# Second mlp: row transposes by VectorE blocks and a DMA through DRAM, in place of TensorE

## The chip, the cores and the metric

The kernel runs on one core of a Trainium2 chip. The metric is the device time of one launch, in microseconds (us). TensorE (PE) does matrix products into PSUM, VectorE (DVE), ScalarE (ACT) and GpSimd (POOL) do elementwise work, and SyncE (SP) issues all DMAs, in the order of its own instruction list. Every engine takes its instructions in order and waits on semaphores for the others.

## The reference

An attention between 512 sequence rows and 32 state rows of each of 8 batch entries makes 8 x (512 + 32) = 4352 token rows of 512 numbers. They pass through two mlps:

```python
def _moe_ref(x, w_gate, w_val, w_out):
    gate = 1.0 / (1.0 + np.exp(-(x @ w_gate)))
    return (gate * (x @ w_val) @ w_out).astype(np.float32)      # 512 -> 1536 -> 512

def _moe2_ref(x, w_in, w_out, g_ln):
    h = x @ w_in                                                # 512 -> 1024
    h_max = np.max(h, axis=-1, keepdims=True)
    e = np.exp(h - h_max)
    sm = e / (np.sum(e, axis=-1, keepdims=True) + 1e-09)
    solu = h * sm
    mu = np.mean(solu, axis=-1, keepdims=True)
    var = np.mean((solu - mu) ** 2, axis=-1, keepdims=True)
    ln = (solu - mu) / np.sqrt(var + 1e-06) * g_ln
    return (ln @ w_out).astype(np.float32)                      # 1024 -> 512
```

Weights and g_ln arrive as float64, and the kernel converts them on the chip.

## The kernel before

Float32 products run as three passes: each operand is split into a high half (a rounded copy) and a low half (the operand less the high half), and `mm3` (L131) sums high x high, low x high and high x low in PSUM. So every matrix product costs three matmuls, and every operand costs one copy for the high half (`hi_of`, ACT, L123) and one subtraction for the low half (`lo_of`, DVE, L129).

Up to about 750 us the kernel does attention, the first mlp (batch row by batch row, in 12 chunks of 128 hidden columns) and the conversion of all weights. Its results, transposed (features on the partitions), go to DRAM (`ysp`). In the last batch row the weights `w_out2` are converted and multiplied by g_ln (`Conv`, L894 and L895).

The second mlp runs over 34 tiles of 128 token rows (`tiles`, L580: eight batch entries of 4 tiles and 2 tiles of state rows). For each tile i:

- `h2` (L610): 24 matmuls of 512 columns for h = x @ w_in, into two of four PSUM banks `acc`, and a DVE maximum of each half.
- `chain` (L616): ACT takes exp of both halves (L621), DVE multiplies by h (L624), makes the statistics (L625, L626) and subtracts the mean (L627) in the tile `eb[i % 3]`. The tile has tokens on the partitions.
- `trans` (L644): the product with `w_out2` needs features on the partitions. Eight TensorE transposes of 128 x 128 (L648) go to the PSUM banks `gps` and `vps`; ACT and DVE split each into high and low halves (`uhl`: the tiles woh9 to woh11, wol9 to wol11, xe2 and xo2).
- `row_scale` (L629): some small DVE operations and two small POOL operations make one factor for each row.
- `out2` (L653): 24 matmuls of 512 columns into `att[i % 2]`; `store` (L661) scales and writes the result.

The loop at L952 issues h2 of tile i, then trans of tile i - 1, chain of tile i, and out2 and store of tile i - 2. Beside it the inputs of the next batch entry are loaded from `ysp` (`y_load`, L590) and split (`y_split`, L595), four pieces for each group of four tiles. In this last loop a scheduler sets the order of each engine's instructions from its own estimate of times; the order is fixed when the kernel is built.

Of the kernel before, what the change touches and what calls it, by code (L numbers as in the profile page):

```python
# [8 lines left out]
F32 = mybir.dt.float32  # L9
# [6 lines left out]
P = 128  # L16
STAGES = 10
WARM = 11
EXPS = 7
# As float32 patterns: float64 high words of 2**-127 and of 2**128.  # L20
EXP_LO = 2.0 ** -15
# [4 lines left out]
def attn_moe_moe2_kernel(ctx: ExitStack, tc: tile.TileContext, x, state, w_gate, w_val, w_out, w_in2, w_out2, g_ln, out):  # L26
    """Float32 products run as float32r passes: each operand is split exactly into hi + lo
    (12 significant bits each) and hi*hi + hi*lo + lo*hi is accumulated in PSUM.

    The weights are float64: their words are taken apart on chip, rounded to float32 and split."""  # L30
    nc = tc.nc
# [24 lines left out]

    # matmul operands
    woh = [f32rt(f"woh{c}", C) for c in range(NF1)]
# [6 lines left out]
    gl = [f32rt(f"gl{i}", S) for i in range(2)]  # L65
    # float32 work tiles
    xn = [f32t(f"xn{g}", 1024) for g in range(2)]
# [18 lines left out]

    # gate's and val's weights of two chunks side by side: first in float32, later split
    wf, wf_pool, xe, xo = {}, {}, {}, {}
    for p in range(NF1 // 2)[::-1]:
        wf_pool[p] = ctx.enter_context(ExitStack())  # L90
        wf[p] = wf_pool[p].enter_context(tc.tile_pool(name=f"sbw{p}", bufs=1)).tile([P, KC, 2, 2, P], F32, name=f"wf{p}")

    def x_pool(p):
        sbx = ctx.enter_context(tc.tile_pool(name=f"sbx{p}", bufs=1, side="right"))
        xe[p], xo[p] = [sbx.tile([P, KC, 2, 2, P], F32R, name=f"{x}{p}") for x in ("xe", "xo")]

    # what only the first row needs
    early = ExitStack()
# [36 lines left out]

# [1 line left out]
    def win(k, f):  # L137
# [9 lines left out]
    class Conv:  # L147
        """Jobs of 512 weights a partition each: load, join the words and, for a pair of
        destination tiles, split.

        `rings` gives the staging and scratch tiles of a job."""

# [6 lines left out]
        def load(self):  # L159
            if not self.jobs:  # L160
                return
            n, src, dst, scale = self.jobs[0]
            i, s = self.rings(n)[0]
            if i in self.held:
                return
            self.jobs.pop(0)
            self.held.add(i)
            v = s.bitcast(U32)
            nc.sync.dma_start(out=v.rearrange("p (k f) -> p k f", k=KC) if len(src.shape) == 3 else v, in_=src)
            self.loaded.append((n, dst, scale))  # L170

        def take(self):
            """Of each word pair: the high word's magnitude, the low word rounded to float32's last place."""
            n, dst, scale = self.loaded.pop(0)
# [14 lines left out]
        def bits(self, n=1):  # L189
            """The high word as float32's bits, kept within float32's range of exponents."""  # L190
            jobs = self.taken[:n]
            for _, _, _, _, t, _, _ in jobs:
                vec.tensor_scalar(out=t, in0=t, scalar1=EXP_LO, scalar2=EXP_HI, op0=ALU.max, op1=ALU.min)  # L193
            for _, _, _, _, t, _, _ in jobs:
                tu = t.bitcast(U32)
                vec.tensor_scalar(out=tu, in0=tu, scalar1=3, scalar2=0x3FFFFFFF, op0=ALU.logical_shift_left, op1=ALU.bitwise_and)  # L196

        def sign(self, n=1):
            """The high word's sign and upper exponent bit."""
            jobs, self.taken = self.taken[:n], self.taken[n:]  # L200
# [37 lines left out]

# [1 line left out]
    def stf(a):  # L240
# [21 lines left out]
    def load_xq(a, g):  # L262
        """x in 32 x 32 blocks, for the transposes of the Vector engine."""
        for q in range(2):
# [8 lines left out]
    def a_state_mm(a, o):  # L273
        """The states transposed, head pairs block diagonal."""
        for j in range(4):
            nc.tensor.transpose(o[:, 64 * j:64 * j + 64], stf(a)[:, j, :], ident[0:64, 0:64])
# [12 lines left out]
    def a_state_pair_split(a, o):  # L289
        if paired(a) and a % 2 == 0:  # L290
            # side by side, in turn the one row's and the other's first
            v = o.rearrange("p (r k e n) -> p r k e n", r=2, k=2, e=2)
# [23 lines left out]
    def a_scores_t(a, g, o, xt):  # L316
        """With the sequence on the partitions."""
        for q in range(2):
# [6 lines left out]

    # softmax over the states, of 16 rows a partition
    def rows_t(g):
# [25 lines left out]
    def a_cols(g):  # L353
        # softmax over the sequence
        m = st2[g]
# [12 lines left out]
    def exps():  # L368
        for g in range(2):
            rows_exp(g)  # L370
        for g in range(2):
            a_cols_exp(g)
        # brings the sigmoid's table back before it is waited for
        act(stat[0][:, 0:1], half, AF.Sigmoid)
# [27 lines left out]
    def a_sread_scale(o):  # L402
        """For probabilities not divided by their sums yet."""
        for g in range(2):
# [27 lines left out]
    def attention(a):  # L432
        """Attention of batch row a by chunks: what the Tensor engine does, and what the others do after it."""
        o = att[1 - a % 2]
# [36 lines left out]

# [1 line left out]
    def ps_acc(m, n):  # L473
        return acc[m][:, 0:n]

    # Of a batch row, xread @ w is taken as attention @ (state @ w), with state @ w = [head and state, ff].
    def put(src, h, l, hi=hi_of):
# [19 lines left out]
    def state_w(b, p, g, i, o, hi, o2=vps):  # L497
        """Of two chunks, half of the heads."""
        n = 2 * p + g
# [6 lines left out]
        elif b % 2 == 0:  # L506
            # the next row's go to DRAM until it is their turn
            for q, o in enumerate((gps, o2)):
# [15 lines left out]
    def state_w1(c, o=gps, t=slice(0, 2), hi=hi_of):  # L524
        """Of one chunk for the first row, all heads, to the ring's first two."""
        p, e = divmod(c, 2)
# [10 lines left out]
    def first_mm(b, c, t, i, parts=range(2)):  # L537
        """From the operands i and i + 1 of the ring for a batch row, from the weights for the state's part."""
        o = (gps, vps)[t]
# [37 lines left out]

# [1 line left out]
    order = [B - 1, 0, SREAD] + list(range(1, B - 1))  # L579
# [15 lines left out]
    def y_split(q, k):  # L595
        n = S if order[q] < B else SR
        h, l = yhl(q, k)
        put(yf[q % 2][k][:, 0:n], h[:, 0:n], l[:, 0:n])

# [16 lines left out]
    def chain(i):  # L616
# [9 lines left out]
        vec.bn_aggr(out=s[:, 4:6], in_=s[:, 8:20])  # L626
        vec.tensor_scalar(out=u, in0=u, scalar1=s[:, 4:5], scalar2=None, op0=ALU.subtract)  # L627

    def row_scale(i):  # L629
        # r / sqrt(r^2 var + 1e-6) with r = 1 / (sum + 1e-9)  # L630
        s = stat[i % 4]
# [8 lines left out]
    def uhl(i, q):  # L640
        n = 2 * (i % 2) + q
        return (woh[9 + n], wol[9 + n]) if n < 3 else (wpart(xe, 2, 0), wpart(xo, 2, 0))

    def trans(i):  # L644
        u = eb[i % 3]
        for q, o in ((0, gps), (1, vps)):
            for j in range(4):
                nc.tensor.transpose(o[:, j * P:(j + 1) * P], u[:, (4 * q + j) * P:(4 * q + j + 1) * P], ident)  # L648
            h, l = uhl(i, q)
            hi_of(h, o)  # L650
            lo_of(l, o, h)

# [19 lines left out]

# [1 line left out]
    def job(c, t):  # L674
# [15 lines left out]

    # the operands of a batch row's gate and val, made ahead: state @ w by halves of pairs of chunks
    ring = [(b, p, g) for b in blocks[1:] if b < B for p in range(NF1 // 2) for g in range(2)]
# [10 lines left out]
    def loads(n):  # L703
        """What the next ones to be made need from DRAM."""
        nonlocal loaded
# [8 lines left out]
    def a_next(b):  # L714
        """The operand of the next block's first products."""
        if b < B:
# [8 lines left out]

    # the first row, with the weights converted just ahead of their use
    with tc.manual_schedule():
# [73 lines left out]

        # by chunk: what the Tensor engine does, and what the others do after it
        parts = [
# [25 lines left out]

        # The chunk with the exponentials keeps the Activation engine busy: its weights are taken  # L830
        # before, some of its other work is left to the next one.
        ahead = {4: 3, 5: 3, EXPS: 0}
# [53 lines left out]
    with tc.manual_schedule():  # L886
        for n_b, b in enumerate(blocks[1:], 1):
# [5 lines left out]
            if last:  # L893
                nc.sync.dma_start(out=glnt, in_=g_ln.rearrange("(j p) -> p j", p=P))  # L894
                conv = Conv([(rows(w_out2, j), (woh[j], wol[j]), glnt[:, j:j + 1]) for j in range(NF2)], rings)  # L895
                conv.load()
# [52 lines left out]
    assert not conv.jobs and not conv.loaded and not conv.joined and made - NF1 == len(ring)  # L949

    nt = len(tiles)
    for i in range(nt):  # L952
# [56 lines left out]
```

## Time and profile before

| | us |
|---|---|
| three runs | 1166.27, 1166.33, 1169.63 |
| their median | 1166.33 |
| span of the profiled execution, first to last instruction | 1163.8 |
| median less span | 2.5 |
| PE busy | 1134.3 (97% of the span) |
| DVE busy | 731.3 (63%) |
| ACT busy | 522.4 (45%) |
| POOL busy | 182.8 (16%) |

The page does not give the total time of the profiled execution apart from its span; the 2.5 us stand for what lies before and after it. A matmul's end is modelled and matmuls overlap, so "busy" on PE says that it had work, not that it was at its peak. The second mlp fills the stretch from about 760 us to the end.

### The profile page before, as it was taken

To read this page: it belongs to the slowest core of one execution; us is meant where nothing else is said; L and a number is where in the kernel's file an instruction comes from. 1 tells how busy PE (TensorE), PEld (TensorE's weight loads), DVE (VectorE), ACT (ScalarE), POOL (GpSimd) and SP (SyncE) were. 2 spreads that over 40 slices of the span, in tenths; PEclk is the share of its full clock that TensorE was granted. 3 is DMA by queue.
4 is the path that set the end of the run, shared out by engine and by line. 5 is a ranking of instruction groups with operands and counts; after the bars stand their busy time and mean duration, and the time that the engine had idled before them with its cause. 6 is when DMAs were issued, how large, how long until landed. Compare 5 with 4: busy or idle time off the path is not lost.

```text
span 1163.8 us, 15755 instructions
## 1 busy us (share of the span) xinstructions
PE 1134.3 (97%) x5847; PEld 906.0 (78%) x5847; DVE 731.3 (63%) x1376; ACT 522.4 (45%) x1002; POOL 182.8 (16%) x205
## 2 busy tenths in 40 slices
PE   7878999999999999999999999999999999999998
PEld 5555667778778778788788988888888888888887
DVE  6999765475564574654754557684675665656553
ACT  6766455654443554445544446532333333332232
POOL 2777533300000000000000422110000000000000
PEclk8999999999999999999999999999999999999999
DMA  9762220331532412603314343120110110000001
GB/s 241 239 200 91 52 60 1 83 85 37 150 93 57 99 35 72 168 19 86 82 37 133 110 151 113 55 69 28 55 55 28 55 64 19 22 25 19 28 19 37
DMA packets 116077, 89.32 MB, mean 77 GB/s; under 512 B 68000, under 2 KB 91808, under 8 KB 116000
## 3 DMA queue, kind: packets, MB, share of 16 engines
q1 hardware_dynamic: 116000, 88.31, 26.6%
q8 instruction: 46, 0.75, 0.3%
q14 instruction: 31, 0.25, 0.1%
HBM read 61.54 MB, written 26.74 MB: 76 GB/s over the span
## 4 chain that ended last, share of the span: by engine, by line
PE 85%; DVE 10%; issue 2%; POOL 1%; ACT 1%; DMA 1%; SPq 1%; POOLq 0%; DVEq 0%; ACTq 0%
PE acc L132 13%; PE acc L134 12%; PE acc L133 12%; PE att L132 6%; PE att L133 6%; PE att L134 6%; PE gps L132 4%; PE gps L133 4%; PE gps L134 4%; PE vps L132 4%; PE vps L134 4%; PE vps L133 4%; DVE wf L203 2%; DVE wf L193 1%; DVE wf L196 1%
## 5 line engine op out<-in xcount | busy, mean ns | idle before, releaser
L132 PE MATMUL acc<-gh,woh 128*128 128x512 f32 (+1 forms) x432 | 168.7, 390 | 0.0
L133 PE MATMUL acc<-gl,woh 128*128 128x512 f32 (+1 forms) x432 | 166.3, 385 | 1.7 <-POOL gl L560 1.3
L554 DVE TENSOR_TENSOR sg<-vps,sg 128x512 f32<-128x512 f32 (+1 forms) x108 | 71.2, 659 | 151.1 <-PE vps L134 137.1
L134 PE MATMUL acc<-gh,wol 128*128 128x512 f32 (+1 forms) x432 | 165.7, 383 | 0.0
L550 ACT ACTIVATE sg<-gps 128x512 f32<-128x512 f32 (+1 forms) x108 | 61.8, 572 | 160.9 <-PE gps L134 156.4
L132 PEld LDWEIGHTS acc<-gh,woh 128*128 128x128 f32 x432 | 82.5, 191 | 32.0 <-issue 15.6
L614 DVE TENSOR_REDUCE stat<-acc 128x1 f32<-128x512 f32 x68 | 46.8, 689 | 92.7 <-PE acc L134 92.7
L133 PEld LDWEIGHTS acc<-gl,woh 128*128 128x128 f32 x432 | 82.3, 190 | 18.5 <-POOL gl L560 2.5
L134 PEld LDWEIGHTS acc<-gh,wol 128*128 128x128 f32 x432 | 82.3, 190 | 15.9
L123 ACT ACTIVATE gh<-sg 128x512 fp32r<-128x512 f32 (+1 forms) x101 | 60.5, 599 | 49.5 <-DVE sg L554 49.4
L133 PE MATMUL att<-wol,woh 128*128 128x512 f32 (+1 forms) x204 | 80.4, 394 | 0.0
L132 PE MATMUL gps<-ah,mh 128*128 128x512 f32 x192 | 75.8, 395 | 4.2 <-DVE ml L129 3.0
L132 PE MATMUL att<-woh,woh 128*128 128x512 f32 (+1 forms) x204 | 79.7, 391 | 0.0
L134 PE MATMUL att<-woh,wol 128*128 128x512 f32 (+1 forms) x204 | 79.5, 390 | 0.0
L637 POOL TENSOR_TENSOR stat<-stat,half 128x1 f32<-128x1 f32 x34 | 18.7, 550 | 379.8 <-DVE stat L636 373.6
L129 DVE TENSOR_TENSOR ml<-gps,mh 64x512 fp32r<-64x512 f32 (+2 forms) x57 | 38.7, 678 | 63.0 <-ACT stg L123 50.9
L132 PE MATMUL vps<-ah,mh 128*128 128x512 f32 x192 | 75.4, 393 | 1.1 <-DVE ml L129 1.1
L133 PE MATMUL gps<-al,mh 128*128 128x512 f32 x192 | 75.3, 392 | 0.7 <-DVE al L129 0.7
L134 PE MATMUL gps<-ah,ml 128*128 128x512 f32 x192 | 75.2, 392 | 0.1
L134 PE MATMUL vps<-ah,ml 128*128 128x512 f32 x192 | 75.2, 392 | 0.0
L560 DVE TENSOR_TENSOR gl<-sg,gh 128x512 fp32r<-128x512 f32 (+1 forms) x97 | 68.1, 702 | 10.9 <-ACT gh L123 6.9
L133 PE MATMUL vps<-al,mh 128*128 128x512 f32 x192 | 75.0, 390 | 0.0
(283 smaller groups left out, 2578.0 us busy)
## 6 DMA issues: line engine op xcount, KB each, us to landing
msp<-stg SPq DMA_DIRECT2D x72, 128.0 KB, 2.3
stg<-msp SPq DMA_DIRECT2D x36, 256.0 KB, 3.0
xn<-in_x_dram SPq DMA_DIRECT2D x15, 512.0 KB, 4.9
e2t<-in_x_dram SPq DMA_DIRECT2D x96, 64.0 KB, 2.6
stge<-in_moe_w_out_dram SPq DMA_DIRECT2D x10, 512.0 KB, 3.7
stge<-in_moe_w_gate_dram SPq DMA_DIRECT2D x9, 512.0 KB, 5.0
stge<-in_moe_w_val_dram SPq DMA_DIRECT2D x9, 512.0 KB, 4.9
xn<-in_moe_w_in_dram SPq DMA_DIRECT2D x8, 512.0 KB, 3.6
```

The lines of the kernel that those rows point to most:

```text
L123: return act(dst, src, AF.Copy)
L129: return vec.tensor_tensor(out=dst, in0=src, in1=r(hi), op=ALU.subtract)
L132: mm(o, lh, rh, start=start, stop=False)
L133: mm(o, lh, rl, start=False, stop=False)
L134: return mm(o, ll, rh, start=False, stop=stop)
L193: vec.tensor_scalar(out=t, in0=t, scalar1=EXP_LO, scalar2=EXP_HI, op0=ALU.max, op1=ALU.min)
L203: vec.scalar_tensor_tensor(out=tu, in0=hi, scalar=0xC0000000, in1=tu, op0=ALU.bitwise_and, op1=ALU.bitwise_or)
L550: act(sg[c % 2][:, 0:n], gps[:, 0:n], AF.Sigmoid)
L554: vec.tensor_tensor(out=g, in0=vps[:, 0:n], in1=g, op=ALU.mult)
L560: eng.tensor_tensor(out=gl[c % 2][:, 0:n], in0=sg[c % 2][:, 0:n], in1=r(gh[c % 2][:, 0:n]), op=ALU.subtract)
L614: vec.tensor_reduce(out=stat[i % 4][:, f:f + 1], in_=h2_out(i, f), axis=AX.X, op=ALU.max)
L637: pool.tensor_tensor(out=s[:, 7:8], in0=s[:, 7:8], in1=half, op=ALU.pow)
```

## The change

Three things change in the second mlp.

The row transposes: for all tiles but the last two, DVE transposes the tile in blocks of 32 x 32 within its place (one instruction of 128 x 1024), one DMA writes the result to a DRAM tile `usp`, and four DMAs read it back so that block rows and block columns change places, each for 32 partitions. The features of a chunk are then not 128 neighbours but 4 groups of 32 that lie 256 apart, so the rows of `w_out2` and g_ln are loaded in that order: 4 DMAs of 32 partitions where one of 128 stood. The last two tiles keep TensorE transposes.

Low halves: those of the transposed rows move from DVE (reading PSUM) to POOL (reading SBUF), and so do those of the second mlp's inputs (`y_split`).

The mean: it is subtracted by ACT, as mean less value, in place of DVE; the sign is given back by g_ln times -1, one small DVE operation at L929 of the changed kernel.

```diff
+            if isinstance(src, list):
+                for b, part in enumerate(src):
+                    nc.sync.dma_start(out=v[32 * b:32 * b + 32], in_=part)
...
     def y_split(q, k):
         n = S if order[q] < B else SR
-        h, l = yhl(q, k)
-        put(yf[q % 2][k][:, 0:n], h[:, 0:n], l[:, 0:n])
+        h, l = [x[:, 0:n] for x in yhl(q, k)]
+        y = yf[q % 2][k][:, 0:n]
+        hi_of(h, y)
+        pool.tensor_tensor(out=l, in0=y, in1=r(h), op=ALU.subtract)
...
         vec.bn_aggr(out=s[:, 4:6], in_=s[:, 8:20])
-        vec.tensor_scalar(out=u, in0=u, scalar1=s[:, 4:5], scalar2=None, op0=ALU.subtract)
+        if i < nt - 2:
+            act(u, u, AF.Identity, bias=s[:, 4:5], scale=-1.0)
+        else:
+            v = ub[i % 2].rearrange("p (q b j) -> p b q j", b=4, q=NF2)
+            act(v, u.rearrange("p (b q j) -> p b q j", b=4, q=NF2), AF.Identity, bias=s[:, 4:5], scale=-1.0)
...
     def trans(i):
         u = eb[i % 3]
-        for q, o in ((0, gps), (1, vps)):
-            for j in range(4):
-                nc.tensor.transpose(o[:, j * P:(j + 1) * P], u[:, (4 * q + j) * P:(4 * q + j + 1) * P], ident)
+        if i >= nt - 2:
...
+            return
+        v, w, d = ub[i % 2], ut[i % 2], usp[i % 3]
+        vec.transpose(out=v, in_=u)
+        nc.sync.dma_start(out=d, in_=v)
+        for b in range(4):
+            nc.sync.dma_start(
+                out=w[32 * b:32 * b + 32].rearrange("p (a e) -> p a e", a=4),
+                in_=d.rearrange("(a j) (b e) -> b j a e", a=4, b=4)[b],
+            )
+        wv = w.rearrange("p (a q i) -> p q a i", a=4, q=NF2)
+        for q in range(2):
             h, l = uhl(i, q)
-            hi_of(h, o)
-            lo_of(l, o, h)
+            hv, lv = [x.rearrange("p (q a i) -> p q a i", q=4, a=4) for x in (h, l)]
+            hi_of(hv, wv[:, 4 * q:4 * q + 4])
+            pool.tensor_tensor(out=lv, in0=wv[:, 4 * q:4 * q + 4], in1=r(hv), op=ALU.subtract)
...
-                nc.sync.dma_start(out=glnt, in_=g_ln.rearrange("(j p) -> p j", p=P))
-                conv = Conv([(rows(w_out2, j), (woh[j], wol[j]), glnt[:, j:j + 1]) for j in range(NF2)], rings)
+                for i in range(4):
+                    nc.sync.dma_start(out=glnt[32 * i:32 * i + 32], in_=g_ln.rearrange("(b q j) -> b j q", b=4, q=NF2)[i])
+                vec.tensor_scalar(out=glnt, in0=glnt, scalar1=-1.0, scalar2=None, op0=ALU.mult)
+                w2 = w_out2.rearrange("(b q j) f -> q b j f", b=4, q=NF2)
+                conv = Conv([([w2[j, b] for b in range(4)], (woh[j], wol[j]), glnt[:, j:j + 1]) for j in range(NF2)], rings)
```

`ub` (2 tiles), `ut` (2) and `usp` (3, in DRAM) are new; the scheduler orders the loop anew. Three places of that order follow. Each row has the line in that kernel, the operation, and out<-in with buffer numbers at the end of a name.

ACT, about one tile and a half in the middle of the second mlp, before (L621 exp, L664 store, L123 high half):

```order
L621 ACTIVATE xn_96,stat_122<-acc_172,stat_122 128x512
L621 ACTIVATE xn_96,stat_122<-acc_173,stat_122 128x512
L664 ACTIVATE stg_107<-att_177,stat_124 128x512
L621 ACTIVATE stg_108,stat_123<-acc_170,stat_123 128x512
L621 ACTIVATE stg_108,stat_123<-acc_171,stat_123 128x512
L123 ACTIVATE woh_72<-gps 128x512
L123 ACTIVATE xe_1205<-vps 128x512
L664 ACTIVATE sg_105<-att_176,stat_121 128x512
```

ACT, the same place in the changed kernel (L630 exp, L126 high half of the rows read back into ut, L638 mean less value, L697 store):

```order
L630 ACTIVATE xn_95,stat_122<-acc_172,stat_122 128x512
L630 ACTIVATE xn_95,stat_122<-acc_173,stat_122 128x512
L126 ACTIVATE woh_70<-ut_5798 128x512
L126 ACTIVATE woh_71<-ut_5798 128x512
L638 ACTIVATE xn_95<-xn_95,stat_122 128x1024
L697 ACTIVATE stg_107<-att_177,stat_124 128x512
L630 ACTIVATE xn_96,stat_123<-acc_170,stat_123 128x512
L630 ACTIVATE xn_96,stat_123<-acc_171,stat_123 128x512
```

The high halves of the tile before (ut) now stand between a tile's exp and its subtraction of the mean.

SP in the second mlp, before (L593 loads from ysp, L666 output):

```order
L666 DMA out_dram<-sg_106 128x512
L666 DMA out_dram<-stg_107 128x512
L593 DMA tt_99<-ysp_184 128x512
L593 DMA tt_100<-ysp_184 128x512
L593 DMA ee_101<-ysp_184 128x512
L593 DMA ee_102<-ysp_184 128x512
L666 DMA out_dram<-stg_107 128x512
```

SP at the same loads in the changed kernel (L673 the write to usp, L675 the four reads, L600 loads from ysp, L699 output):

```order
L699 DMA out_dram<-stg_107 128x512
L673 DMA usp_5802<-ub_5796 128x1024
L675 DMA ut_5798<-usp_5802 32x4x256 x4
L600 DMA tt_99<-ysp_184 128x512
L600 DMA tt_100<-ysp_184 128x512
L600 DMA ee_101<-ysp_184 128x512
L600 DMA ee_102<-ysp_184 128x512
L699 DMA out_dram<-stg_107 128x512
L673 DMA usp_5800<-ub_5797 128x1024
```

Each tile now has one write and four reads between its output and the next; the loads from ysp stand behind the reads of one tile and ahead of the write of the next.

PE near the end, before (L648 transposes of the last tile, L132 to L134 matmuls of out2):

```order
L132 MATMUL att_176<-woh_67,woh_71 128x512
L648 MATMUL gps<-ident,xn_95 128x128 x4
L648 MATMUL vps<-ident,xn_95 128x128 x4
L133 MATMUL att_176<-wol_79,woh_71 128x512
L134 MATMUL att_176<-woh_67,wol_83 128x512
L132 MATMUL att_176<-woh_68,woh_71 128x512
L133 MATMUL att_176<-wol_80,woh_71 128x512
L134 MATMUL att_176<-woh_68,wol_83 128x512
L132 MATMUL acc_170<-woh_61,woh_72 128x256
```

PE near the end of the changed kernel (L666 transposes of the last tile, L135 to L137 matmuls):

```order
L135 MATMUL att_176<-woh_68,woh_71 128x512
L136 MATMUL att_176<-wol_80,woh_71 128x512
L137 MATMUL att_176<-woh_68,wol_83 128x512
L666 MATMUL gps<-ident,ub_5797 128x128 x4
L666 MATMUL vps<-ident,ub_5797 128x128 x4
L135 MATMUL acc_170<-woh_61,woh_72 128x256
```

The last tile's transposes stood five matmuls ahead of the end of the second last out2; they now stand behind it.

## Rows read from the trace of the kernel before

**Rows 1.** The page: busy time by engine; the clock granted, in 40 slices.
```profile
PE 1134.3 (97%) x5847; PEld 906.0 (78%) x5847; DVE 731.3 (63%) x1376; ACT 522.4 (45%) x1002; POOL 182.8 (16%) x205
...
PEclk8999999999999999999999999999999999999999
```

**Rows 2.** Windows: stretch and its length, busy us by engine, clock, DMA share, GB/s.
```profile
765.00:775.00 10.00, 10.00 (x49) 8.18 (x48) 9.34 (x25) 3.98 (x10) 0.75 (x2) 1.00 0.29 101
949.08:1045.14 96.06, 96.06 (x451) 78.75 (x449) 58.96 (x136) 30.14 (x64) 5.95 (x16) 1.00 0.09 33
```

**Rows 3.** Chain that ended last: start us, us, what; the first tile is eight before the last.
```profile
949.08 0.44 PE gps L648 x4
949.52 0.44 PE vps L648 x4
...
1045.14 0.44 PE gps L648 x4
```

**Rows 4.** Timeline, one tile from its last h2 matmul: start us, us, engine, line, operation.
```profile
961.65 0.40 PE L134 MATMUL acc<-xe,gl 128*128 128x512 f32 x1
962.09 0.69 DVE L614 TENSOR_REDUCE stat<-acc 128x1 f32<-128x512 f32 x1 [2.11 <-PE acc L134]
963.00 0.69 ACT L621 ACTIVATE xn<-acc,stat 128x512 f32<-128x512 f32 x1 [5.78 <-DVE stat L619]
```

**Rows 5.** Timeline, the tile before: exp, and DVE up to the subtraction of the mean.
```profile
953.47 0.69 ACT L621 ACTIVATE stg<-acc,stat 128x512 f32<-128x512 f32 x1 [2.14 <-DVE stat L619]
956.99 0.21 DVE L626 BATCH_NORM_AGGREGATE stat<-stat 128x2 f32<-128x12 f32 x1
957.23 0.76 DVE L627 TENSOR_SCALAR stg<-stg,stat 128x1024 f32<-128x1024 f32 x1
```

**Rows 6.** Groups of lines by form: count, busy us, mean ns of one, idle before.
```profile
L310 DVE STREAM_TRANSPOSE xtr<-e2t 128x512 f32<-128x512 f32 x24 | 15.7, 687 | 2.1 <-DMA e2t<-in_x_dram 2.1
L129 DVE TENSOR_TENSOR wol<-vps,woh 128x512 fp32r<-128x512 f32 x13 | 8.8, 680 | 0.0
L492 POOL TENSOR_TENSOR xo<-wf,xe 128x512 fp32r<-128x512 f32 x24 | 31.6, 1337 | 55.1 <-ACT xe L123 55.1
```

**Rows 7.** Tile e2t: ACT copies from SBUF, ns min/median/max, first and last start, form.
```profile
L123 ACT ACTIVATE gh<-e2t x8: 620/632/635, 753.8 to 998.7; 128x512 fp32r<-128x512 f32 x8
```

**Rows 8.** DMA issues: KB each, median us from issue to landing.
```profile
out_dram<-sg SPq DMA_DIRECT2D x15, 256.0 KB, 2.0
xn<-in_moe_w_out_dram SPq DMA_DIRECT2D x8, 512.0 KB, 3.5
xn<-in_x_dram SPq DMA_DIRECT2D x15, 512.0 KB, 4.9
out_dram<-sg SPq DMA_DIRECT2D x8, 64.0 KB, 1.7
xn<-ssp SPq DMA_DIRECT2D x1, 512.0 KB, 3.9
ee<-ysp SPq DMA_DIRECT2D x2, 128.0 KB, 2.5
glnt<-in_moe_g_ln_dram SPq DMA_DIRECT2D x1, 4.0 KB, 3.3
```

**Rows 9.** Timeline of SP: issues, back to back in the second row.
```profile
673.25 0.43 SPq L894 DMA_DIRECT2D glnt<-in_moe_g_ln_dram  x1
755.39 0.92 SPq L593 DMA_DIRECT2D e2t<-ysp  x2
```

**Rows 10.** Timeline of DVE: the work ahead of where L929 of the changed kernel stands.
```profile
685.87 0.41 DVE L560 TENSOR_TENSOR gl<-sg,gh 128x256 fp32r<-128x256 f32 x1
```

**Rows 11.** Timeline, the last tile's transposes and the matmuls behind them.
```profile
1153.14 0.60 PE L648 MATMUL vps<-ident,xn 128*128 128x128 f32 x4
1153.34 0.60 ACT L123 ACTIVATE woh<-gps 128x512 fp32r<-128x512 f32 x1 [4.02 <-PE gps L648]
1153.50 0.48 PE L133 MATMUL att<-wol,woh 128*128 128x512 f32 x1
```

More of the change, by code (lines that the diff above doesn't have):

```diff
@@ L91, in attn_moe_moe2_kernel @@
         wf[p] = wf_pool[p].enter_context(tc.tile_pool(name=f"sbw{p}", bufs=1)).tile([P, KC, 2, 2, P], F32, name=f"wf{p}")
+    x_late = ctx.enter_context(ExitStack())
     def x_pool(p):
-        sbx = ctx.enter_context(tc.tile_pool(name=f"sbx{p}", bufs=1, side="right"))
+        sbx = (ctx if p < 3 else x_late).enter_context(tc.tile_pool(name=f"sbx{p}", bufs=1, side="right"))
         xe[p], xo[p] = [sbx.tile([P, KC, 2, 2, P], F32R, name=f"{x}{p}") for x in ("xe", "xo")]
@@ L168, in load @@
             v = s.bitcast(U32)
-            nc.sync.dma_start(out=v.rearrange("p (k f) -> p k f", k=KC) if len(src.shape) == 3 else v, in_=src)
+            if isinstance(src, list):
+                for b, part in enumerate(src):
+                    nc.sync.dma_start(out=v[32 * b:32 * b + 32], in_=part)
+            else:
+                nc.sync.dma_start(out=v.rearrange("p (k f) -> p k f", k=KC) if len(src.shape) == 3 else v, in_=src)
             self.loaded.append((n, dst, scale))
@@ L626, in chain @@
         vec.bn_aggr(out=s[:, 4:6], in_=s[:, 8:20])
-        vec.tensor_scalar(out=u, in0=u, scalar1=s[:, 4:5], scalar2=None, op0=ALU.subtract)
+        if i < nt - 2:
+            act(u, u, AF.Identity, bias=s[:, 4:5], scale=-1.0)
+        else:
+            v = ub[i % 2].rearrange("p (q b j) -> p b q j", b=4, q=NF2)
+            act(v, u.rearrange("p (b q j) -> p b q j", b=4, q=NF2), AF.Identity, bias=s[:, 4:5], scale=-1.0)
     def row_scale(i):
@@ L645, in trans @@
         u = eb[i % 3]
-        for q, o in ((0, gps), (1, vps)):
-            for j in range(4):
-                nc.tensor.transpose(o[:, j * P:(j + 1) * P], u[:, (4 * q + j) * P:(4 * q + j + 1) * P], ident)
+        if i >= nt - 2:
+            for q, o in ((0, gps), (1, vps)):
+                for j in range(4):
+                    nc.tensor.transpose(o[:, j * P:(j + 1) * P], ub[i % 2][:, (4 * q + j) * P:(4 * q + j + 1) * P], ident)
+                h, l = uhl(i, q)
+                hi_of(h, o)
+                lo_of(l, o, h)
+            return
[9 more added lines that the diff above has]
+        for q in range(2):
             h, l = uhl(i, q)
-            hi_of(h, o)
-            lo_of(l, o, h)
+            hv, lv = [x.rearrange("p (q a i) -> p q a i", q=4, a=4) for x in (h, l)]
+            hi_of(hv, wv[:, 4 * q:4 * q + 4])
+            pool.tensor_tensor(out=lv, in0=wv[:, 4 * q:4 * q + 4], in1=r(hv), op=ALU.subtract)
     def out2(i, js=range(NF2), d=slice(0, DO), bank=None):
@@ L949, in attn_moe_moe2_kernel @@
     assert not conv.jobs and not conv.loaded and not conv.joined and made - NF1 == len(ring)
+    x_late.close()
+    sbu = ctx.enter_context(tc.tile_pool(name="sbu", bufs=1, side="right"))
+    ub = [sbu.tile([P, 1024], F32, name=f"ub{i}") for i in range(2)]
+    ut = [sbu.tile([P, 1024], F32, name=f"ut{i}") for i in range(2)]
+    usp = [tc.dram_tile([P, 1024], F32, name=f"usp{i}") for i in range(3)]
     nt = len(tiles)
```

## The prediction

> **What bounds the kernel now.** I read the page first: PE is busy for 97% of the span at the full granted clock, and no other engine passes 63% [rows 1]. That is an average, so the second look went to the stage that is changed: in a stretch of eight tiles PE is busy in all 96.06 us, DVE in 58.96, ACT in 30.14 and POOL in 5.95 [rows 2]. The chain of waits, third, runs through PE alone there; the reader should see that the transposes stand in it as two pieces of four, 0.44 us each (0.435 from start to start), and that eight tiles lie between 949.08 and 1045.14 [rows 3]. So a tile takes 96.06 / 8 = 12.01 us, all of it PE's, and whatever PE sheds is gained, as long as nothing else takes longer than what is left. Last I followed one tile through the timeline, to see how late each step comes after its h2.
>
> **What is taken from PE.** 34 tiles have eight transposes each; 32 tiles lose them. A tile's eight cost 2 x 0.435 = 0.87 us [rows 3], so 32 x 0.87 = 27.8 us go, and a tile becomes 12.01 - 0.87 = 11.14 us of PE.
>
> **What moves between the other engines.** DVE loses two low halves of 0.68 us a tile [rows 6], the mean's 0.76 [rows 5] and one input's low half of about the same 0.68, and gets one transpose of 1024 columns. The trace has it only for 512 columns, at 0.687 us [rows 6]; between that and twice that I take 1.3, nearer to twice, since the columns double. From 58.96 / 8 = 7.4 us a tile DVE falls to 7.4 - 2.1 - 0.7 + 1.3 = 5.9. ACT has 3.8 a tile and gets the mean: a copy of 512 columns from SBUF takes 0.63 [rows 7], so 0.63 to 1.26 for 1024, I take 1.15; it stands at 4.9. POOL gets three subtractions of 512 columns at 1.34 [rows 6]: 0.7 + 4.0 = 4.7. All three stay far under 11.14, so by load alone every one of these edits is hidden behind PE. If that cover went, POOL's 4.0 would be the dearest.
>
> **The new round trip.** This is where it can fail. A tile's rows now go from ACT (mean) to DVE (transpose) to SP (write), to SP (four reads), to ACT (two high halves), to POOL (two low halves), to PE. And the order of ACT puts the high halves of tile i - 1 ahead of the mean of tile i. So if the rows of i - 1 come late, the mean of i waits for them, its rows come as late again, and a loop closes: mean, transpose, write, reads, two high halves, next mean. Its length L stands against 11.14.
>
> - Mean 1.15 and transpose 1.3, as above.
> - Write of 512 KB. A write of 64 KB lands after 1.7 us, one of 256 KB after 2.0, and a read of 512 KB in long runs after 3.5 [rows 8]. Between 2.0 and 3.5 I take 2.7, nearer to the writes.
> - Four reads of 128 KB. One lands after 2.5 [rows 8]; two issues take SP 0.92 [rows 9], so the fourth goes out 3 x 0.46 = 1.4 later and lands at 3.9, which is also what the one read of 512 KB in short runs took (xn from ssp). At best all come within 2.5, at worst as the 512 KB of x do, 4.9 [rows 8].
> - Two high halves, 2 x 0.63 = 1.26 [rows 7].
> - Four handovers. A matmul ends at 962.05 and DVE starts at 962.09 [rows 4], so 0.04 at best; I take 0.1 each, 0.4.
>
> L = 1.15 + 1.3 + 2.7 + 3.9 + 1.26 + 0.4 = 10.7 us. From the low ends it is 0.63 + 0.69 + 2.0 + 2.5 + 1.26 + 0.2 = 7.3, from the high ends 1.26 + 1.37 + 3.5 + 4.9 + 1.26 + 0.5 = 12.8. At 10.7 PE stays the bound, with 0.4 us a tile to spare, and the margin is what I am least sure of.
>
> The Trainium skill ("DMA: Bandwidth & Descriptors", Anatomy of one DMA) gives a DMA about 2.0 us fixed, most of it the wait for the receipt from the target memory, and its bytes at 436 GB/s. The rows of 64 and 256 KB lie a little under that. By it the write would take 3.2 and a read 2.3, and L would be 11.0: the margin all but gone, and with it some weight on the second rival below.
>
> Is a tile also early enough? In a tile, exp starts 0.95 us after the last h2 matmul ends [rows 4], and the mean is ready 957.20 - 953.47 = 3.7 after exp starts [rows 5], so the mean can go 4.7 us after the end of h2. The high halves of the tile before are done 4.7 + 10.7 - 11.14 = 4.3 after that same point: just before they would be in the way. The rows reach ACT at 4.7 + 9.4 = 14.1, the first low half is made by 14.1 + 0.6 + 0.1 + 1.3 = 16.1, and out2 starts two tiles after its h2, at 22.3. So PE has 6 us of cover. What is queued behind the waiting instructions: on ACT the mean and the store of the tile before last, on DVE (behind the transpose) the maxima of the next tile, which are ready only 8.4 us after (half of out2 and of h2: three quarters of 11.14), on SP the next output. Once every four tiles ACT makes four input copies (2.5 us) and POOL their low halves (5.3 us), behind the store, and the four loads from ysp wait on SP for POOL behind a tile's reads; by the same clock POOL is done about 3 us into the next tile and the next write is asked for at about 7.4, so they fit, with some jitter inside the 6 us.
>
> **Start and end.** At the start the order runs h2 of tiles 0 to 3 and half of 4 before the first out2, some 20 us that cover the first round trip. DVE, at 5.9 a tile against 5.6 of h2 alone, may lag; it is nearly full there already (9.34 of 10 us [rows 2]). Between nothing and 4 us I take 1.0. At the end the last tile's transposes have lost the five matmuls behind them. Before, PE went on at 1153.50 with these while ACT copied from 1153.34 to 1153.94 [rows 11]. Now it waits for that copy (0.4) and then some for DVE's low half: 0.7 us. In the first mlp's last block the load of g_ln becomes four issues and DVE waits for them at once. SP starts them at 673.25 and they land by 673.25 + 4 x 0.43 + 3.3 = 678.3 [rows 8, 9]; DVE comes there after 685.87 [rows 10], so this costs nothing, with 8 us to spare. The weights' loads in four parts are asked for two chunks ahead: nothing.
>
> **The sum**, against the profiled execution: 1163.8 - 27.8 + 1.0 + 0.7 = 1137.7 us of span. The median lies 2.5 above that span, so 1140.2. A clock that falls is not in it: the stages of the first mlp that are matmuls alone keep the full clock in the same page [rows 1].
>
> **Rivals.**
>
> *The loop is longer than the tile was, and the kernel gets slower.* Place: the mean on ACT behind the high halves that come back through DRAM. Tiles 6 to 31, 26 of them, run at L once the 6 us of cover are used up. It costs 26 x (L - 11.14) - 6, which eats the 26.1 us net gain at L = 12.4; from there it is slower. At the high ends, 12.8, the time is 1140.2 + 43 - 6 = 1177. For it: two DMAs in a row with a receipt between, four issues, none of it in the trace in this form. Against it: three of the four parts must lie at their worst at once. The Trainium skill's rule to use TensorE for 128 x 128 transposes where PSUM will do, VectorE having only 32 x 32 blocks ("VectorE: DVE Perf Modes", Rules for kernel authors), would come true in this way. Chance 0.15.
>
> *The loop lies between the new tile and the old one, or the lumps of four inputs break it.* L of 11.6 gives 26 x 0.46 - 6 = 6 us back, 1146; L of 12.1 gives 19 back, 1159. Lumps that cost PE 2 us for each of seven groups give 14 back, 1154. For it: the thin margin; against it: the 6 us of cover, which the 0.4 us a tile restore. Chance 0.20, nearly all of it still faster.
>
> *The transposes are hidden anyway, or the start eats the gain*, about the old time. The chain shows them on PE with no idle beside them, so I give this 0.03.
>
> **How the numbers follow.** PE stays the bound: 0.62, likeliest, 1136 to 1146 (nothing lost at start and end gives 1138.5, and the runs shown lie 3.4 apart, so a little below that). Range 1136 to 1165: it takes in this and the second rival, and leaves out the slower one and what lies below, under 0.2. A measurement of this kernel can tell 0.3%, 3.5 us, from no change. Faster by more than that: 0.62 and 0.17 of the second rival, 0.79; within: 0.06; slower: 0.15.
>
> **What would show it.** PE busy in all of a stretch of eight tiles of 89.1 us; no L648 rows but for two tiles. The read-back landing under 4 us and the write under 3; the mean on ACT released by DVE's statistics. If it is released by a DMA landing instead, the loop closes, and L can be read off as the distance of two means. A PE that waits for POOL at every out2 would make the forecast wrong, as would DVE waiting on the mean while PE waits for DVE's maxima.

## The result, and the profile after

The changed kernel takes 1139.94 us (median of 4 runs, 1138.34 to 1141.43), against 1167.07 for the kernel before on the same chip (4 runs). The ratio is 0.977, with an interval of 0.9755 to 0.979. The profiled execution took 1138.34 with a span of 1136.4, so 1.9 lies outside the span here. The 2.5 that the forecast added was the median of the runs less the span of another, faster execution; the runs of the kernel before that list their own span have 1.7 to 1.9 outside it. The forecast was 1140.2, with a span of 1137.7.

The page of the changed kernel, busy time by engine and the granted clock (before: [rows 1]):

```profile
PE 1103.1 (97%) x5591; PEld 876.4 (77%) x5591; DVE 692.8 (61%) x1279; ACT 556.8 (49%) x1036; POOL 300.9 (26%) x301
...
PEclk9999999999999999999999999999999999999999
```

PE has 256 matmuls fewer, which is 32 tiles of eight, and is busy for the same share of a shorter span. Windows of the second mlp, then of the end (stretch and length, busy us of PE, PEld, DVE, ACT and POOL, clock, DMA share, GB/s; before: [rows 2]):

```profile
800.00:1100.00 300.00, 300.00 (x1295) 242.94 (x1294) 165.70 (x378) 128.33 (x241) 117.38 (x131) 1.00 0.39 130
1120.00:1130.00 10.00, 9.49 (x56) 8.05 (x55) 2.06 (x8) 3.39 (x5) 0.74 (x2) 1.00 0.15 54
```

PE is full for 300 us, so PE is still the bound. 27 tiles lie in this window: DVE has 165.70 / 27 = 6.1 us a tile, ACT 4.8 and POOL 4.3. How long a tile is now, in PE's timeline: the first h2 matmul of a tile, and the same eight tiles later (start us, us, engine, line, operation):

```profile
963.22 0.40 PE L135 MATMUL acc<-xe,ah 128*128 128x512 f32 x1
...
1052.28 0.40 PE L135 MATMUL acc<-xe,ah 128*128 128x512 f32 x1
```

Eight tiles take 89.06 us, 11.13 each; before they took 96.06, 12.01 each [rows 3].

Now one turn of the round trip. The timeline of ACT, then DVE, SP and POOL for the same microseconds (in brackets the idle time before a row and what ended it):

```profile
954.43 0.63 ACT L126 ACTIVATE woh<-ut 128x512 fp32r<-128x512 f32 x1 [5.25 <-DMA ut<-usp]
954.97 0.61 ACT L126 ACTIVATE xe<-ut 128x512 fp32r<-128x512 f32 x1
955.49 1.14 ACT L638 ACTIVATE xn<-xn,stat 128x1024 f32<-128x1024 f32 x1
...
965.20 1.15 ACT L126 ACTIVATE woh<-ut 128x512 fp32r<-128x512 f32 x2 [4.39 <-DMA ut<-usp]
966.26 1.14 ACT L638 ACTIVATE xn<-xn,stat 128x1024 f32<-128x1024 f32 x1
...
956.66 1.25 DVE L672 STREAM_TRANSPOSE ub<-xn 128x1024 f32<-128x1024 f32 x1 [4.63 <-ACT xn L638]
...
957.93 0.34 SPq L673 DMA_DIRECT2D usp<-ub  x1
960.63 1.74 SPq L675 DMA_DIRECT2D ut<-usp  x4
...
965.91 1.29 POOL L684 TENSOR_TENSOR wol<-ut,woh 128x512 fp32r<-128x512 f32 x1 [7.45 <-ACT woh L126]
```

Read it as a chain. The mean starts at 955.49, the transpose at 956.66, the write at 957.93, the reads at 960.63, the high halves at 965.20, and the next mean at 966.26: 1.17 + 1.27 + 2.70 + 4.57 + 1.06 = 10.77 us. ACT stands idle until the rows have come back through DRAM, and only then does the next mean. This is the closed loop of the prediction, and it turns in 10.77 us against PE's 11.13. What the other engines wait for between 800 and 1100 (us in total, times, longest):

```profile
POOL wol L684 <- ACT woh L126: 169.4, 26, 9.5
ACT woh L126 <- DMA ut<-usp: 97.5, 27, 5.3
DVE ub L672 <- ACT xn L638: 50.4, 16, 4.6
```

In the same stretch the list has no row of PE. The other engines do wait, but nothing that PE needs comes late.

### The profile page after: what moved, and what is told of

It reads as the page before. It is cut to its first block, busy times and chain, and to the rows that moved or that the text cites. A ratio compares the mean times of both kernels' runs of the same rounds, so it can differ in the third digit from the quotient of the medians.

```text
span 1136.4 us, 15718 instructions
## 1 busy us (share of the span) xinstructions
PE 1103.1 (97%) x5591; PEld 876.4 (77%) x5591; DVE 692.8 (61%) x1279; ACT 556.8 (49%) x1036; POOL 300.9 (26%) x301
## 4 chain that ended last, share of the span: by engine, by line
PE 84%; DVE 10%; issue 2%; ACT 1%; POOL 1%; DMA 1%; SPq 1%; DVEq 0%; POOLq 0%; ACTq 0%
PE acc L135 13%; PE acc L137 13%; PE acc L136 13%; PE att L135 6%; PE att L136 6%; PE att L137 6%; PE gps L135 4%; PE gps L136 4%; PE gps L137 4%; PE vps L135 4%; PE vps L137 4%; PE vps L136 4%; DVE wf L210 2%; DVE wf L200 2%; DVE wf L203 1%
## 5 line engine op out<-in xcount | busy, mean ns | idle before, releaser
L135 PE MATMUL acc<-gh,woh 128*128 128x512 f32 (+1 forms) x432 | 168.2, 389 | 0.0
L137 PE MATMUL acc<-gh,wol 128*128 128x512 f32 (+1 forms) x432 | 164.9, 382 | 0.0
L684 POOL TENSOR_TENSOR wol<-ut,woh 128x512 fp32r<-128x512 f32 x48 | 61.4, 1293 | 192.1 <-ACT woh L126 184.8
L135 PEld LDWEIGHTS acc<-gh,woh 128*128 128x128 f32 x432 | 82.0, 190 | 32.0 <-issue 15.6
L137 PEld LDWEIGHTS acc<-gh,wol 128*128 128x128 f32 x432 | 81.8, 189 | 15.6
L126 ACT ACTIVATE gh<-sg 128x512 fp32r<-128x512 f32 (+1 forms) x101 | 60.5, 599 | 49.3 <-DVE sg L561 49.3
L126 ACT ACTIVATE woh<-ut 128x512 fp32r<-128x512 f32 x48 | 28.6, 627 | 107.7 <-DMA ut<-usp 107.2
L135 PE MATMUL gps<-ah,mh 128*128 128x512 f32 x192 | 75.6, 394 | 4.5 <-DVE ml L132 3.3
L135 PE MATMUL att<-woh,woh 128*128 128x512 f32 (+1 forms) x204 | 79.5, 390 | 0.0
L137 PE MATMUL att<-woh,wol 128*128 128x512 f32 (+1 forms) x204 | 79.0, 387 | 0.0
L132 DVE TENSOR_TENSOR ml<-gps,mh 64x512 fp32r<-64x512 f32 (+2 forms) x57 | 38.6, 678 | 63.0 <-ACT stg L126 50.8
L220 POOL TENSOR_TENSOR tt<-tt,xn 128x512 int32<-128x512 int32 x16 | 20.9, 1307 | 211.3 <-DVE tt L210 197.6
L135 PE MATMUL vps<-ah,mh 128*128 128x512 f32 x192 | 75.2, 392 | 1.1 <-DVE ml L132 1.1
L126 ACT ACTIVATE mh<-gps 64x512 fp32r<-64x512 f32 (+2 forms) x53 | 31.3, 590 | 90.6 <-PE gps L137 60.4
L137 PE MATMUL gps<-ah,ml 128*128 128x512 f32 x192 | 75.0, 391 | 0.1
```

What stands on the lines that cost most here:

```text
L126: return act(dst, src, AF.Copy)
L132: return vec.tensor_tensor(out=dst, in0=src, in1=r(hi), op=ALU.subtract)
L135: mm(o, lh, rh, start=start, stop=False)
L137: return mm(o, ll, rh, start=False, stop=stop)
L220: pool.tensor_tensor(out=ti, in0=ti, in1=lo, op=ALU.add)
L684: pool.tensor_tensor(out=lv, in0=wv[:, 4 * q:4 * q + 4], in1=r(hv), op=ALU.subtract)
```

## The experiments

### The moves without the transposes

All 34 tiles keep their TensorE transposes. What is left of the change is its moves: the mean on ScalarE, the low halves of the inputs on GpSimd, the new order of the weights. The rows' low halves then stay on VectorE, since they are made from PSUM.

```diff
+DMA_TILES = 0
...
-        if i < nt - 2:
+        if i < DMA_TILES:
...
-        if i >= nt - 2:
+        if i >= DMA_TILES:
```

> The transposes stay on TensorE for all 34 tiles; only the rest of the change stands: the mean on ACT, the inputs' low halves on POOL, the rows of w_out2 in the new order. If PE is the bound and only the transposes on it count, the time is that of the kernel before, 1167 us within 3, and PE is busy without a gap over eight tiles of 96 us. If the gain came from the relief of VectorE (7.4 to about 5 us a tile), a large part of the 27 us is here already, 1140 to 1155.

Measured: 1167.46 us, 1.0009 of before (0.9998 to 1.002). Windows of this kernel, the same columns:

```profile
949.00:1045.00 96.00, 96.00 (x449) 78.66 (x448) 48.42 (x120) 38.60 (x73) 16.03 (x24) 1.00 0.10 34
```

DVE is relieved of 10 us in these 96, ACT and POOL carry them, and nothing is gained: PE is full as before [rows 2].

### Half of the tiles

The same switch at 16.

```diff
-DMA_TILES = 0
+DMA_TILES = 16
```

> 16 of the 34 tiles go through DRAM, 18 keep TensorE. If each tile moved is worth 0.87 to 0.90 us of PE and nothing else, 16 of 32 parts of the gain are left: 1140 + 16 x 0.88 = 1154 us, 1152 to 1156. If the gain is a matter of the start or the end of the second mlp, it is 1140 or 1167.

Measured: 1152.80 us, 0.9885 (0.9871 to 0.99). Sixteen tiles are worth 1166.5 - 1152.8 = 13.7 us, 0.86 each; all 32 are worth 27.1, 0.85 each. The gain goes with the number of tiles that lose their TensorE transposes.

### The transposes alone

The DMA path stays, and everything that moved goes back to VectorE: the mean, the rows' low halves, the inputs' low halves.

```diff
-        pool.tensor_tensor(out=l, in0=y, in1=r(h), op=ALU.subtract)
+        vec.tensor_tensor(out=l, in0=y, in1=r(h), op=ALU.subtract)
...
-            act(u, u, AF.Identity, bias=s[:, 4:5], scale=-1.0)
+            vec.tensor_scalar(out=u, in0=u, scalar1=s[:, 4:5], scalar2=-1.0, op0=ALU.subtract, op1=ALU.mult)
...
-            pool.tensor_tensor(out=lv, in0=wv[:, 4 * q:4 * q + 4], in1=r(hv), op=ALU.subtract)
+            vec.tensor_tensor(out=lv, in0=wv[:, 4 * q:4 * q + 4], in1=r(hv), op=ALU.subtract)
```

> The transposes alone: as the changed kernel, but the mean, the rows' low halves and the inputs' low halves are all on VectorE, as before. VectorE then has 7.4 - 0.7 + 1.25 and so about 8 us of a tile's 11.1, and ACT's high halves no longer stand ahead of a mean. If PE is the bound, 1140 us within 3. If the moves to POOL and ACT were needed to hide the work, VectorE falls behind and the time is 1145 to 1165.

Measured: 1150.20 us, 0.9867 (0.9849 to 0.9884): 10 us of the gain are lost. The window of the 300 us, the same columns:

```profile
800.00:1100.00 300.00, 296.25 (x1252) 234.21 (x1251) 207.42 (x457) 95.45 (x205) 20.93 (x51) 0.99 0.39 127
```

DVE's timeline around one transpose of this kernel, and PE's row that waits there:

```profile
946.88 0.67 DVE L634 BATCH_NORM_STATS2 stat<-stg 128x6 f32<-128x512 f32 x1
949.32 0.69 DVE L684 TENSOR_TENSOR wol<-ut,woh 128x512 fp32r<-128x512 f32 x1 [1.76 <-ACT woh L126]
...
950.59 0.20 DVE L635 BATCH_NORM_AGGREGATE stat<-stat 128x2 f32<-128x12 f32 x1
950.82 0.75 DVE L638 TENSOR_SCALAR stg<-stg,stat 128x1024 f32<-128x1024 f32 x1
...
951.61 1.25 DVE L672 STREAM_TRANSPOSE ub<-stg 128x1024 f32<-128x1024 f32 x1
...
949.34 0.50 PE L135 MATMUL att<-woh,woh 128*128 128x512 f32 x1 [0.83 <-ACT woh L126]
```

DVE is busy for 207 of 300 us, so it isn't full. But its order puts the low halves of tile i - 1 (L684) between the statistics of tile i and its mean. DVE has made the statistics, stands idle for 1.76 us until the rows of i - 1 are back and ACT has copied them, and only then goes on to the mean and the transpose. The loop is closed here too, through DVE, and it is longer: the means of the last 26 tiles that go through DRAM lie 11.69 us apart, (1113.31 - 820.94) / 25, where PE needs 11.13. PE waits ahead of its out2 and issues 1252 matmuls in a stretch in which the changed kernel issues 1295. A part of the loss came with the clock: from 1040 to 1060, where PE waited longest (2.3 us), the granted clock was 0.91 as a mean and matmuls followed each other by 0.43 us from 1056 to 1060, not 0.23; in the stretches beside it the clock was 1.00.

### Only the rows' low halves moved

Two of the three edits of the last kernel are kept (mean and inputs' low halves on VectorE), and L684 is on GpSimd again.

```diff
-            vec.tensor_tensor(out=lv, in0=wv[:, 4 * q:4 * q + 4], in1=r(hv), op=ALU.subtract)
+            pool.tensor_tensor(out=lv, in0=wv[:, 4 * q:4 * q + 4], in1=r(hv), op=ALU.subtract)
```

> Beside the changed kernel: the mean of the rows and the low halves of the inputs go back from ScalarE and GpSimd to VectorE, and only the low halves of the rows (L684) stay on GpSimd. Theory (the kernel with everything left on VectorE took 1150 because the rows' low halves stand in VectorE's order between a tile's statistics and its transpose, and there wait for the landing of the reads; VectorE's load has no part in it): 1140 within 2, TensorE fully busy from 800 to 1100. Rival (it is VectorE's load: the low halves of inputs and rows and the mean weigh alike): about half of the 10 us come back at most, 1144 to 1150, with TensorE idle in the tiles that load the inputs.

Measured: 1140.22 us, 0.9779 (0.9766 to 0.9792), the time of the changed kernel. The window:

```profile
800.00:1100.00 300.00, 300.00 (x1296) 242.94 (x1295) 201.00 (x426) 102.07 (x216) 89.06 (x107) 1.00 0.40 131
```

DVE is as busy as in the kernel before it (201.00 against 207.42), and PE is full. So it was not DVE's load: this kernel and the one before it differ in one line, the engine of L684. Of the three moves one was needed, the one whose operation waits for the round trip, and it had to leave the engine on which the next tile's transpose is queued.

### The mean on VectorE, in the changed kernel

This opens the loop. The mean no longer stands behind the high halves on ACT.

```diff
-            act(u, u, AF.Identity, bias=s[:, 4:5], scale=-1.0)
+            vec.tensor_scalar(out=u, in0=u, scalar1=s[:, 4:5], scalar2=-1.0, op0=ALU.subtract, op1=ALU.mult)
```

> As the changed kernel, but the mean is subtracted by VectorE (same sign), so that it no longer waits behind the high halves of the tile before, and the loop over DRAM is open. The time stays at 1140 us within 3 if the loop cost PE nothing; in the trace the subtraction then follows the statistics at once in every tile, some 5 us after the end of h2, where it came 4.9 to 8.9 us after before. If PE did lose time to the loop, it is 2 to 6 us faster.

Measured: 1139.89 us, 0.9776 (0.9759 to 0.9793). DVE's timeline of one tile:

```profile
963.49 0.21 DVE L635 BATCH_NORM_AGGREGATE stat<-stat 128x2 f32<-128x12 f32 x1
963.73 0.75 DVE L638 TENSOR_SCALAR xn<-xn,stat 128x1024 f32<-128x1024 f32 x1
964.40 0.15 DVE L648 TENSOR_TENSOR stat<-stat 128x1 f32<-128x1 f32 x1
964.52 1.25 DVE L672 STREAM_TRANSPOSE ub<-xn 128x1024 f32<-128x1024 f32 x1
```

The mean follows the statistics at once and the transpose follows it: the loop is gone, and the time is the same. So the closed loop of the changed kernel costs nothing.

### A longer loop, closed and open

Two kernels with the same dearer read-back: eight reads of 64 KB in place of four of 128 KB. In the first the mean of tile i is held behind the high halves of tile i - 1 for every tile, also at the start, where the changed kernel's order does not do this. In the second the mean is on VectorE, as above.

```diff
+            with tc.issue_after(high[i - 1].ins) if i - 1 in high else ExitStack():
+                act(u, u, AF.Identity, bias=s[:, 4:5], scale=-1.0)
...
+            for j in range(2):
+                nc.sync.dma_start(
+                    out=w[32 * b + 16 * j:32 * b + 16 * j + 16].rearrange("p (a e) -> p a e", a=4),
+                    in_=d.rearrange("(a j) (b e) -> b j a e", a=4, b=4)[b, 16 * j:16 * j + 16],
+                )
```

> The rows are read back by 8 DMAs of 64 KB in place of 4 of 128 KB, and the mean of a tile is held behind the high halves of the tile before, as the order of the changed kernel has it. Four more issues of 0.43 us make the loop about 1.7 us longer: 10.7 becomes 12.4 undisturbed, and some 12.8 with the input loads, over the 11.1 us of PE. If the loop then sets the pace, 26 tiles lose 1.7 us each less 6 us of cover: 1140 + 38 = 1178 us, 1165 to 1185, and TensorE idles before out2. If the loop does not matter (PE alone counts, and DMA latency is hidden), 1140 us within 4.

> The same 8 DMAs, but the mean on VectorE, so that the loop is open and the rows are only 1.7 us later in each tile. Out2 starts two tiles after h2, with 6 us of cover, so 1140 us within 3 by the loop theory. If what hurts with 8 reads is the DMA work itself (SyncE's issues, the queue, contention), it is as slow as the kernel with the loop closed.

Measured: closed 1177.93 us, 1.0088 of before (1.0071 to 1.0106); open 1144.33 us, 0.9811 (0.9793 to 0.9829). The same reads, 33.6 us apart. The closed kernel's window:

```profile
800.00:1100.00 300.00, 286.89 (x1210) 224.82 (x1209) 150.32 (x351) 118.45 (x220) 109.99 (x123) 1.00 0.37 122
```

One of its two groups of means, the one with the first and the last of all 32 (ns min/median/max, first and last start):

```profile
L639 ACT ACTIVATE xn<-xn,stat x22: 1132/1134/1154, 769.6 to 1147.5; 128x1024 f32<-128x1024 f32 x22
```

One turn in its timeline, ACT, then SP, then PE:

```profile
941.43 0.63 ACT L126 ACTIVATE woh<-ut 128x512 fp32r<-128x512 f32 x1 [4.82 <-DMA out_dram<-sg]
...
942.49 1.13 ACT L639 ACTIVATE stg<-stg,stat 128x1024 f32<-128x1024 f32 x1
...
954.34 1.13 ACT L639 ACTIVATE xn<-xn,stat 128x1024 f32<-128x1024 f32 x1
...
944.93 0.32 SPq L674 DMA_DIRECT2D usp<-ub  x1
947.55 3.60 SPq L677 DMA_DIRECT2D ut<-usp  x8
...
942.12 0.50 PE L135 MATMUL att<-woh,woh 128*128 128x512 f32 x1 [0.61 <-ACT woh L126]
```

The 32 means are 31 distances, (1147.5 - 769.6) / 31 = 12.19 us, longer than PE's 11.13, and PE waits for the halves that are made from the reads. What PE waited for in the closed kernel between 800 and 1100 (us in total, times, longest), POOL's low halves more often than ACT's high halves:

```profile
PE att L137 <- POOL wol L686: 10.7, 16, 1.8
PE att L135 <- ACT woh L126: 2.1, 3, 1.0
```

Eight issues keep SP for 3.60 us in place of 1.74. (ACT's wait is put down to the output's DMA, which is short; its copy reads what the eight reads bring.) This is the mechanism of the slower rival, brought about by the edit, and it does make the kernel slower than before, by 0.9%. That 1177.93 falls on the forecast of 1178 is in part luck. The turn above, from 942.49 to 954.34, takes 11.85, not 12.4; in return more tiles than the 26 run at the loop's pace, the first mlp ends later (below), and behind PE's longest wait, 5.4 us at 1129, the granted clock was 0.68 from 1130 to 1140 and 0.84 from 1140 to 1150. The kernel does not measure the rival's break-even of 12.4, since the edit closes the loop in the first tiles too: the mean at 806.9 is the fourth tile's here, and at 806.7 in the changed kernel it is the sixth's.

The open kernel's median is 4.4 us above the changed one's, more than the 3 allowed. The two profiled executions lie 6.4 us apart (spans of 1142.8 and 1136.4), and most of that arises ahead of the second mlp. A group of products of the first mlp (count, ns min/median/max, first and last start), in the changed kernel:

```profile
L137 PE MATMUL gps<-ah,ml x192: 388/389/501, 18.7 to 744.6; 128*128 128x512 f32 x192
```

The same group in the open kernel, then in the closed one:

```profile
L137 PE MATMUL gps<-ah,ml x192: 388/389/628, 21.9 to 748.5; 128*128 128x512 f32 x192
L137 PE MATMUL gps<-ah,ml x192: 387/389/628, 23.5 to 749.9; 128*128 128x512 f32 x192
```

The open kernel is 3.2 us late at the first of them and 3.9 at the last, the closed one 4.8 and 5.3, before the second mlp begins, in code that the edits do not touch. Why the start is later stays open. So the second mlp of the open kernel is 2.5 us longer than that of the changed one. Between 800 and 1100 its PE is busy for 299.68; most of the rest is one wait of PE near the end (us in total, times, longest):

```profile
PE gps L666 <- ACT ub L641: 1.6, 1, 1.6
```

The last two tiles keep TensorE transposes and their mean is still on ACT (L641). The first of the two means stands behind the high halves of the last tile that came through DRAM, and PE, which is to transpose its result, waits for it. Of the loop one turn is left there.

## Why the prediction was right

**The bound.** It held as the prediction had it: PE was the bound in the second mlp, and what it shed was gained. The moves alone give nothing, half of the tiles give half, all give all.

**What is taken from PE.** Predicted 0.87 us a tile, 27.8 in all. A tile went from 12.01 to 11.13, which is 0.88, and 32 of them are 28.

**The loop.** Predicted 10.7, in parts; one turn of the trace gives 10.77. The mean was 1.14 (1.15 predicted) and the transpose 1.25 (1.3). The write is released after 2.70 (2.7); its median landing is 2.6. The reads were mis-sized: 4.57 from the first issue to the high halves, in place of 3.9, since a read of 128 KB landed after 2.9 as a median, not 2.5 [rows 8], with three more issues of 0.43 ahead of the last. Two high halves in a row take 1.06, not 1.26, and a handover some 0.03, not 0.1. That the errors nearly cancel is luck: with 4.57 for the reads and the other terms as predicted, the sum would have been 11.3, above PE's 11.14. The DMA issues of the changed kernel (KB each, median us to landing):

```profile
usp<-ub SPq DMA_DIRECT2D x32, 512.0 KB, 2.6
ut<-usp SPq DMA_DIRECT2D x128, 128.0 KB, 2.9
```

From the Trainium skill's split ("DMA: Bandwidth & Descriptors", Anatomy of one DMA) the prediction estimated 3.2 for the write and 2.3 for a read. The page fits that split to DMAs issued from GpSimd, and these are issued from SyncE. Here it is not borne out: the large write was faster (2.6) and the small reads, four at a time, slower (2.9). The sum by it, 11.0, would have left the same verdict.

**What the prediction said would show.** PE full in a stretch of eight tiles of 89.1: 89.06. Write under 3 and single reads under 4: yes. But the mean is mostly not released by DVE's statistics: it stands right behind the high halves, which were released by a DMA. The loop is closed, as the prediction's own test reads it. Of its 26 turns between 806.68 and 1097.57, 14 take 10.66 to 10.92 us and ten take 11.27 to 12.83. The lumps of four inputs, which the prediction feared, are not the reason: three of the six turns with input copies on ACT take 10.69 to 10.79, and in seven of the ten long turns no input is loaded or copied. SP's rows of the longest turn and of another long one:

```profile
831.75 0.32 SPq L673 DMA_DIRECT2D usp<-ub  x1
836.46 1.74 SPq L675 DMA_DIRECT2D ut<-usp  x4
...
865.29 1.74 SPq L704 DMA_DIRECT2D out_dram<-sg  x4
867.13 0.38 SPq L673 DMA_DIRECT2D usp<-ub  x1
```

In the longest the reads go out 4.71 us behind the write, not 2.70; in the tiles whose means start at 863.56 and 875.46 the write stands on SP behind the four outputs of a tile of state rows and goes out 2.4 us after the transpose starts, not 1.27; in the turn from 943.52 the high halves come 5.78 us after the reads, not 4.57. Why single writes and reads land late stays open. So the means slip against h2 (4.7 us after the end of its last matmul at 806.68, as predicted, and 8.8 at 955.49; counted from the next matmul's start, as in the expectation above, 4.9 and 8.9) and catch up again. The twelve turns from 817.84 to 955.49 take 11.47 each, longer than PE's tile. The slip used up to 4.1 of the 6 us of cover that the prediction had, and PE never felt it. That is the second rival's mechanism, at work inside the cover, and the margin was as thin as the prediction feared.

**"By load alone every one of these edits is hidden."** True of the mean and of the inputs' low halves: putting both back costs nothing. It was the wrong question for the rows' low halves. They cost DVE 1.4 us a tile, which it has to spare, but their place in its order closes a longer loop, and leaving them there costs 10 us. By the prediction's own formula the measured 11.69 costs 26 x (11.69 - 11.13) - 6 = 8.6 us, most of the 10. The prediction found such a loop on ACT and did not look for it on DVE, because there the change had already taken it away.

**Start and end.** The start cost nothing in place of 1.0: PE is full from 755 to the last tile's transposes. The prediction's 8.4 us until the next tile's maxima are ready are the whole of out2 and half of h2, not half of each; the figure is right, the words beside it are not. The end, PE's timeline of the last tile's transposes (before: [rows 11]):

```profile
1125.18 0.39 PE L137 MATMUL att<-woh,wol 128*128 128x512 f32 x1
1125.41 0.60 PE L666 MATMUL gps<-ident,ub 128*128 128x128 f32 x4
1125.85 0.60 PE L666 MATMUL vps<-ident,ub 128*128 128x128 f32 x4
1126.90 0.39 PE L135 MATMUL acc<-woh,woh 128*128 128x256 f32 x1 [0.45 <-ACT woh L126]
```

From the second piece to the end it is 1136.4 - 1125.85 = 10.55. Before it was 1163.8 - 1153.14 = 10.66, with five matmuls of 0.23 in it that have now gone ahead. So the end costs 10.55 - (10.66 - 1.15) = 1.0, in place of 0.7. The ledger of spans: 28 - 0 - 1.0 = 27.0 of the measured 1163.8 - 1136.4 = 27.4. The other 0.4 is not the second mlp's: the group of products shown above starts its last one at 744.6 here and at 745.0 in the kernel before. The median comes within 0.3 us of the forecast, which is closer than the terms are: the start was 1.0 too dear, the end 0.3 too cheap, and the 2.5 outside the span 0.6 too high, while the runs of one kernel lie 3 us apart.

**The rule against it.** That 128 x 128 transposes belong on TensorE where PSUM will do (the Trainium skill, "VectorE: DVE Perf Modes", Rules for kernel authors) would have come true with a loop like the closed one above. Here TensorE is the one engine without a free microsecond, and the measurement goes against the rule by 27 us.

No run points to a version clearly below 1140: PE is full, and with the loop open it stays the same. Of what this change costs, the tail is left, about 1 us.

## What to carry to other kernels

When one engine is full, the time of what leaves it is gained, here 0.88 us a tile, even if the work goes by a detour of 10 us, as long as the detour is not a loop longer than the tile and its result is there before it is needed. So list, for each engine on the detour, what stands queued behind the instruction that waits for the detour's end: if that is the detour's own next start, the loop's length counts and not the engine's load, and the cure is to put the waiting instruction on an engine with nothing of the kind behind it.

## What was not expected

In the kernel with the mean on VectorE, DVE and POOL hold each other up. POOL's low halves and DVE's mean in one tile, each engine's timeline:

```profile
952.45 1.29 POOL L684 TENSOR_TENSOR wol<-ut,woh 128x512 fp32r<-128x512 f32 x1 [6.72 <-ACT woh L126]
953.70 1.74 POOL L684 TENSOR_TENSOR xo<-ut,xe 128x512 fp32r<-128x512 f32 x1
...
952.64 1.65 DVE L638 TENSOR_SCALAR xn<-xn,stat 128x1024 f32<-128x1024 f32 x1
954.21 1.24 DVE L648 TENSOR_TENSOR stat<-stat 128x1 f32<-128x1 f32 x1
```

The mean takes 1.65 us where it takes 0.75 alone, POOL's second subtraction 1.74 where it takes 1.29, and an operation on one column 1.24 where it takes 0.15; it ends with POOL's, at 955.4. They end together, as if they took turns. The Trainium skill says the same ("SBUF — State Buffer", Who interferes with whom): VectorE, in some modes or with two SBUF inputs, and GpSimd share a port that one of them holds for a whole instruction. With the mean on ScalarE the changed kernel has little of it: its L684 takes 1.28 to 1.31, and of its 68 operations of this kind on one column (L648, L649) six take 0.35 to 1.29, against 23 in the kernel with the mean on VectorE. In neither kernel does it reach PE.
